# A chunked state-space layer and a gelu MLP on one core: how the first sequence's operands are loaded and turned, and where B by token comes from

## The chip, the cores and the metric

The kernel runs on one core of one Trainium2 chip. The metric is the time of one execution on the device in microseconds (us). The kernel before takes 120.17 us, the median of three runs (119.97 to 120.31).

## What is computed

Two layers follow each other. The first is a state-space scan over 4 sequences (b) of 768 tokens, with 8 heads (H) of width 32 (D) and a state of 16 (N) per head. It is computed in chunks:

```python
log_a = np.log(np.clip(a, 1e-06, 1.0))
for c in range(nc):
    cum = np.cumsum(la, axis=-1)
    L = np.exp(cum[:, :, :, None] - cum[:, :, None, :]) * causal
    M = np.einsum('bhin,bhjn->bhij', Cc, Bc) * L
    y_intra = np.einsum('bhij,bhjd->bhid', M, xc)
    y_inter = np.einsum('bhin,bhnd->bhid', Cc, state) * np.exp(cum)[..., None]
    y[:, :, sl] = y_intra + y_inter
    Bx = np.einsum('bhjn,bhjd->bhjnd', Bc, xc) * np.exp(cum[:, :, -1:] - cum)[..., None, None]
    state = np.exp(np.sum(la, axis=-1))[:, :, None, None] * state + np.sum(Bx, axis=2)
```

The second is an MLP over the 3072 tokens, with the 8 heads side by side as 256 features: `gelu_tanh(y @ w_in) @ w_out`, with w_in 256x2048 and w_out 2048x256. All inputs and the output are float32. The result does not depend on the chunk length; the kernel uses chunks of 128 tokens, 6 per sequence, 24 in all.

## The kernel before, in words

**Units.** The 24 chunks are taken as 13 units: chunk 0, chunk 1, and then pairs. Every function `f_...` issues the instructions of one step for one unit, and its steps are these.

- Decays. Products of `a` from a token to the end of its chunk are formed by a scan on VectorE (`f_R` for sequence 0 and the chunk ends of all, `f_scang` for sequences 1 to 3). B is multiplied by that product and C by its reciprocal (`f_mul0`, `f_mul`, `f_mulg`), so that no matrix of decays is needed.
- B and C are needed with (head, state) on the partitions: `bh` and `ch`. In sequence 0, PE transposes them (`f_T0` for chunk 0, L583; `f_T` for the rest, L604), and ACT copies them out of PSUM (`f_bh0`, `f_E`). In sequences 1 to 3 VectorE does it by its 32x32 block transpose (`f_Tg`, L543). `ce` is C twice, masked to even and odd heads (`f_ce0`, `f_F` L619, `f_Fg` L553).
- G (L659) is B times C, 128x128 for each head, in `gb`; M (L669) is its copy with the causal mask, bfloat16.
- B by token (`bn`) is needed with tokens on the partitions. In every sequence PE transposes `bh` back (`f_N`, L625) and ACT copies the result out (`f_bn`, L458).
- D (L680) is B by token times x, the chunk's addition to the state; S (L728, L730) carries the state on and SP (L737) spreads it out over a block mask `bmask`.
- Y (L702 from the carried state, L711 from M and x) is the layer's output; `f_yev` (L720) copies it to `xm`.
- s1 (L757) is the first stage of the MLP, `f_gelu` (L765) its gelu on ACT, s2 (L774) the second stage; `f_oev` copies the result out and `f_store` (L787) sends it. The last chunk's s2 is done in two halves (L792) in one tile `gb`.

x and the weights are cast to bfloat16 (`f_castx`, `f_wi`, `f_wo`, all through L458 to L462), mostly on GpSimd.

**Order.** The order of the work is not that of the code. Each step is a node with an engine, an estimated duration, the steps that it needs and a priority; `run_order` goes through them as if each engine ran in order, and issues them in the order found. PSUM is scarce: the two `hp` tiles are shared by s1, D and small products, `gb` by G, M and `f_N`, `yb` by Y and some s2. Where the plan has PE idle, before the first s2, `idle` puts products of a zero tile there (L1065).

**Loads.** All loads but two stand in one queue on SP, in this order: `a`; B and C of chunk 0 (64-byte rows); B and C of all of sequence 0 (384-byte rows); x of chunk 0; w_in, a quarter at a time, with x of chunk 1 and of chunks 2 and 3 between; w_out in four quarters; x of chunks 4 and 5; then for each of sequences 1 to 3 `a`, B, C (four loads each), and x. The stores are in the same queue.

```python
load_bc_n()
load_x_n(0)
load_w_n(0, 1)
load_x_n(1)
load_w_n(2, 3)
load_x_n(2)
load_w_n(0, 1, 2, 3, o=True)
load_x_n(3)
```

Of the kernel before, what the change touches and what calls it, by code (L numbers as in the profile page):

```python
# [31 lines left out]
def run_order(nodes, pools, hop=0.08, same=0.04, idle=None, wait=()):  # L32
# [64 lines left out]
    'f_clip(0, 256)': 308.538, 'f_R(0,)': -15.941, 'f_clip(256, 384)': -339.826, 'f_RT0()': 1159.49,  # L97
    'f_R(1,)': 367.141, 'f_recip0()': -323.896, 'f_mul0(1,)': -323.906, 'f_mul0(0,)': -35.176,
    'f_T0(1,)': 1123.21, 'f_T0(0,)': 1159.5, 'f_ce0()': -138.371, 'f_bh0()': 266.725, 'f_R(2,)': 330.337,
    'f_G(0,)': -91.981, 'f_pe()': -193.992, 'f_RT()': 1125.27, 'f_M(0, 0, 0, 2)': -285.936,  # L100
    'f_M(0, 0, 2, 4)': 367.131, 'f_pp()': 1125.26, 'f_recip()': 468.131, "f_castx(0, 'ACT')": 266.715,
    'f_mul(1,)': -194.002, 'f_pend()': 270.364, 'f_Y(0,)': 1119.78, 'f_yev(0,)': 209.42,
    'f_mul(0,)': -35.176, 'f_T(1,)': 1152.81, "f_wi(0, 0, 2, 'POOL')": 97.158,
    "f_E(0, 1, 'ACT', 21, 64)": 270.354, 'f_T(0,)': 55.447, "f_E(0, 1, 'ACT', 64, 128)": 272.36,
    'f_F(0, 128, 384)': 468.121, 'f_D(0,)': 1170.19, 'f_s1(0, 0)': 1244.43,
    "f_E(0, 0, 'ACT', 21, 64)": -152.035, 'f_F(0, 384, 768)': -343.397, "f_wi(1, 0, 2, 'POOL')": 106.043,
    "f_E(0, 0, 'ACT', 64, 128)": 102.425, 'f_S(0, 0)': -318.328, 'f_G(1,)': 1209.63, 'f_SP(0,)': -323.654,
    'f_gelu(0, 0)': 267.9, 'f_N(0,)': 1123.2, "f_castx(1, 'POOL')": 106.053, 'f_M(1, 0, 0, 4)': -287.074,
    'f_s1(0, 1)': 1244.44, "f_bn(0, 'ACT')": 270.405, 'f_D(1,)': 1119.09, 'f_gelu(0, 1)': 103.579,
    'f_G(2,)': 379.65, "f_wi(2, 0, 1, 'POOL')": -96.227, "f_wi(2, 1, 2, 'DVE')": 244.836,  # L110
    'f_S(1, 0)': 509.234, 'f_Y(1,)': 1167.76, 'f_SP(1,)': -318.348, 'f_s1(0, 2)': -68.513,
    'f_yev(1,)': -185.791, "f_wi(3, 0, 1, 'POOL')": 97.168, "f_wi(3, 1, 2, 'DVE')": -166.728,
    'f_gelu(0, 2)': 88.559, 'f_M(2, 0, 0, 4)': 468.111, 'f_s1(0, 3)': 256.892, 'f_s1(1, 0)': -5.424,
    'f_gelu(0, 3)': 841.948, 'f_M(2, 1, 0, 4)': 286.612, "f_castx(2, 'POOL')": 106.083,
    'f_gelu(1, 0)': 209.42, 'f_s1(1, 1)': 1244.44, 'f_D(2,)': -72.563, 'f_gelu(1, 1)': 310.499,
    'f_G(3,)': 1170.77, "f_wo(0, 'POOL')": -6.862, 'f_S(2, 0)': -86.636, 'f_s1(1, 2)': 1167.75,
    'f_SP(2,)': -328.534, 'f_S(2, 1)': -166.718, 'f_Y(2,)': 1125.08, 'f_gelu(1, 2)': -187.491,
    'f_SP(3,)': -95.439, "f_wo(1, 'POOL')": 106.093, 'f_s1(1, 3)': 39.343, 'f_M(3, 0, 0, 4)': 471.605,
    'f_yev(2,)': 310.489, "f_s2(0, 0, 0, 'o')": 1244.43, "f_s2(0, 0, 1, 'o')": 1149.98,
    'f_gelu(1, 3)': 43.879, "f_wo(2, 'POOL')": 71.86, 'f_s1(2, 0)': 262.608, 'f_M(3, 1, 0, 4)': -59.147,  # L120
    'f_s1(2, 1)': 1158.13, 'f_gelu(2, 0)': 316.947, "f_s2(0, 0, 2, 'o')": -169.949,
    "f_wo(3, 'POOL')": -209.595, 'f_gelu(2, 1)': 45.731, 'f_s1(2, 2)': 1170.19, 'f_s1(2, 3)': -203.565,
    'f_gelu(2, 2)': -95.091, "f_s2(0, 0, 3, 'o')": 1161.73, "f_castx(3, 'POOL')": 106.073,
    'f_gelu(2, 3)': -187.501, 'f_s1(2, 4)': -116.936, 'f_clipg(1,)': -328.524, 'f_scang(1,)': -182.29,
    "f_oev(0, 'ACT')": 316.957, 'f_s1(2, 5)': -331.499, 'f_gelu(2, 4)': 69.73, 'f_rT(1,)': 1150.59,
    "f_s2(1, 0, 0, 'o')": -206.245, 'f_qT(1,)': -105.019, "f_s2(1, 0, 1, 'o')": 281.291,
    'f_gelu(2, 5)': -281.439, 'f_D(3,)': -165.791, 'f_s1(2, 6)': 215.528, 'f_mulg(1, 0, 0, 3)': -276.921,
    "f_s2(1, 0, 2, 'o')": 348.67, 'f_S(3, 0)': -197.187, 'f_gelu(2, 6)': -234.888,
    "f_s2(1, 0, 3, 'o')": -86.131, 'f_SP(4,)': -161.739, 'f_s1(2, 7)': -124.52,
    'f_mulg(1, 0, 3, 6)': -104.486, "f_oev(1, 'ACT')": 253.329, 'f_Y(3,)': -102.426, 'f_store(0,)': 1122.82,  # L130
    'f_gelu(2, 7)': -70.863, 'f_Tg(1, 0, 0, 3)': -94.76, "f_s2(2, 0, 0, 'o')": -163.857,
    'f_Tg(1, 0, 3, 6)': -94.74, 'f_yev(3,)': -250.819, "f_s2(2, 0, 1, 'o')": -198.132,
    'f_mulg(1, 1, 0, 3)': -35.543, 'f_N(1,)': -102.426, "f_s2(2, 0, 2, 'o')": -88.02,
    'f_Tg(1, 1, 0, 3)': -42.833, "f_bn(1, 'ACT')": -84.712, 'f_s1(3, 0)': -86.121, 'f_Fg(1, 0, 3)': -153.974,
    'f_s1(3, 1)': -168.693, 'f_gelu(3, 0)': -281.449, 'f_mulg(1, 1, 3, 6)': -29.236,
    "f_s2(2, 0, 3, 'o')": 85.43, 'f_store(1,)': 1190.34, 'f_G(4,)': 280.653, 'f_gelu(3, 1)': 98.272,
    'f_Tg(1, 1, 3, 6)': -105.336, 'f_s1(3, 2)': 281.281, "f_oev(2, 'ACT')": 316.947,
# [115 lines left out]
def kernel(  # L253
# [68 lines left out]
    def load_bc(b, i):  # L322
        d = U[b]
        if "bc" not in d:
            d["bc"] = ld.tile([128, 2, H, R6 * N], FP32, name="bc_t")
# [777 lines left out]
```

## Time and profile before

| what | value |
|---|---|
| median of three runs | 120.17 us |
| profiled execution, its own time | 118.98 us |
| its span (first to last instruction) | 117.0 us |
| granted TensorE clock, mean | 0.995 of full speed |
| first s1 / first s2 on PE | 12.30 / 21.29 us |
| first G / G of chunk 1 / G of chunks 2 and 3 | 6.67 / 13.28 / 15.18 us |
| last product's end / last copy's end | 113.57 / 114.31 us |
| busy PE, DVE, ACT, POOL | 111.7, 71.2, 75.3, 18.1 us |

PE is TensorE, PEld its weight loads, DVE VectorE, ACT ScalarE, POOL GpSimd, SP the engine that issues most DMAs. A busy engine is one that runs any instruction, the zero products included. The profile page gives the busy share of each engine in 40 slices of 2.9 us, as digits in tenths. The chain of waits goes back from the last instruction to what released each one. In the timeline an instruction that waits for another engine inside its execution shows as a longer duration, not as idle time.

### The profile page before, as it was taken

The page shows a single profiled execution, that of the slowest core. Times are in us where ns is not written, and L with a number is a line of the kernel's source. Part 1 is how long each engine was busy: PE and PEld are TensorE (multiplying, and loading weights), DVE is VectorE, ACT ScalarE, POOL GpSimd, SP SyncE. Part 2 cuts the span into 40 slices and gives each one's busy share as a digit, 9 for nine tenths or more (in the row PEclk, how much of TensorE's full clock was granted, in tenths as well). Part 3 has the DMA queues.
Part 4 walks back from the last instruction along what each step waited for, and adds up shares of the span by engine and source line. Part 5 has one row for each costly group of instructions (what it writes and reads, how often), then busy time and mean ns, then how long its engine had stood idle before and what let it go on. Part 6 is the DMA issues. An engine that isn't in the chain of part 4 may idle for free.

```text
span 117.0 us, 3536 instructions
## 1 busy us (share of the span) xinstructions
PE 111.7 (96%) x1484; PEld 98.9 (85%) x1484; DVE 71.2 (61%) x161; ACT 75.3 (64%) x145; POOL 18.1 (16%) x38
## 2 busy tenths in 40 slices
PE   5899999999999999999999999999999999999980
PEld 5788778997987897998989899898989899999970
DVE  3787999939699996994999693291919000000100
ACT  4123756795765778687666859667777776676610
POOL 7303735640032003200510000000000000000000
PEclk9999999999999999999999999999999999999998
DMA  2998979968959497579611101101101101111111
GB/s 49 251 287 233 364 180 375 313 153 188 207 137 218 112 210 169 117 186 208 172 46 45 44 7 45 41 12 45 50 0 45 50 0 44 45 50 45 46 47 45
DMA packets 44251, 14.28 MB, mean 122 GB/s; under 512 B 39052, under 2 KB 42700, under 8 KB 44236
## 3 DMA queue, kind: packets, MB, share of 16 engines
q1 hardware_dynamic: 43148, 13.95, 48.4%
q10 hardware_dynamic: 1088, 0.11, 0.7%
q8 instruction: 11, 0.18, 0.6%
q14 instruction: 4, 0.03, 0.1%
HBM read 10.91 MB, written 3.15 MB: 120 GB/s over the span
## 4 chain that ended last, share of the span: by engine, by line
PE 87%; DVE 7%; POOL 2%; issue 1%; ACT 1%; POOLq 0%; DVEq 0%; ACTq 0%
PE hp L757 35%; PE o_ps L774 31%; PE gb L659 3%; PE yb L774 3%; DVE m L669 3%; PE yb L711 3%; PE yb L702 3%; PE o_ps L1065 2%; PE gb L792 2%; DVE ce L619 1%; PE hp L492 1%; PE gb L625 1%; DVE sp_new L737 1%; DVE w_in_sb L462 1%; PE hp L680 1%
## 5 line engine op out<-in xcount | busy, mean ns | idle before, releaser
L765 ACT ACTIVATE gT<-hp 128x512 bf16<-128x512 f32 x96 | 53.6, 596 | 20.0 <-PE hp L757 19.9
L757 PE MATMUL hp<-xm,w_in_sb 128*128 128x256 bf16 (+1 forms) x416 | 53.0, 267 | 0.0
L757 PEld LDWEIGHTS <-w_in_sb 128*128 128x128 bf16 x416 | 42.0, 115 | 3.3 <-issue 2.1
L774 PE MATMUL o_ps<-w_out_sb,gT 128*128 128x256 bf16 x336 | 44.4, 273 | 0.0
L774 PEld LDWEIGHTS <-gT 128*128 128x128 bf16 x368 | 35.8, 98 | 3.6
L669 DVE TENSOR_TENSOR m<-gb,tri 128x1024 bf16<-128x1024 f32 (+1 forms) x25 | 28.5, 1171 | 0.0
L783 DVE COPY o_sb<-o_ps 128x256 f32<-128x256 f32 x1 | 0.4, 425 | 18.5 <-ACT gT L765 18.5
L781 ACT ACTIVATE o_sb<-o_ps 128x256 f32<-128x256 f32 x20 | 7.7, 386 | 4.9 <-ACT gT L765 3.2
L737 DVE SCALAR_TENSOR_TENSOR sp_new<-s_new,pend,bmask 128x256 bf16<-128x256 f32 x20 | 10.3, 526 | 0.3
L1065 PE MATMUL o_ps<-wz 128*128 128x128 bf16 x75 | 8.9, 281 | 1.3 <-DVE warm L364 1.3
L460 POOL CAST x<-xs_t 128x512 bf16<-128x512 f32 x9 | 5.6, 654 | 27.6 <-DMA xs_t<-in_x_dram 18.1
L730 DVE SCALAR_TENSOR_TENSOR s_new<-s_new,pend,hp 128x64 f32<-128x64 f32 x16 | 4.5, 279 | 7.3 <-PE hp L680 4.4
L720 ACT ACTIVATE xm<-yb 128x512 bf16<-128x512 f32 (+1 forms) x13 | 7.3, 563 | 2.4 <-PE yb L711 2.2
L1065 PEld LDWEIGHTS <-wz 128*128 128x128 bf16 x75 | 6.9, 129 | 1.6 <-DVE warm L364 1.3
L711 PE MATMUL yb<-m,x 128*32 128x128 bf16 x192 | 6.3, 223 | 0.0
L702 PE MATMUL yb<-ce,sp_new 128*32 128x128 bf16 x160 | 5.3, 221 | 0.0
L659 PE MATMUL gb<-ce,bh 32*128 32x256 bf16 x96 | 5.2, 282 | 0.1
L533 DVE TENSOR_TENSOR bc<-bc_t,rr 128x192 bf16<-128x192 f32 x12 | 4.6, 435 | 1.0 <-DMA bc_t<-in_C_dram 0.9
L460 POOL CAST w_in_sb<-wf 128x512 bf16<-128x512 f32 x6 | 3.7, 636 | 8.4 <-DMA wf<-in_moe_w_in_dram 8.4
L460 POOL CAST w_out_sb<-wf 128x1024 bf16<-128x1024 f32 x4 | 4.2, 1040 | 2.4 <-DMA wf<-in_moe_w_out_dram 2.4
L711 PEld LDWEIGHTS <-x 128*32 128x32 bf16 x192 | 3.8, 97 | 0.8 <-issue 0.8
L702 PEld LDWEIGHTS <-sp_new 128*32 128x32 bf16 x160 | 2.9, 96 | 1.7 <-issue 1.6
(83 smaller groups left out, 67.3 us busy)
## 6 DMA issues: line engine op xcount, KB each, us to landing
out_dram<-o_sb SPq DMA_DIRECT2D x23, 128.0 KB, 1.8
xs_t<-in_x_dram SPq DMA_DIRECT2D x3, 768.0 KB, 6.6
wf<-in_moe_w_in_dram SPq DMA_DIRECT2D x4, 512.0 KB, 7.0
wf<-in_moe_w_out_dram SPq DMA_DIRECT2D x4, 512.0 KB, 6.4
bc_t<-in_B_dram SPq DMA_DIRECT2D x12, 96.0 KB, 2.8
bc_t<-in_C_dram SPq DMA_DIRECT2D x12, 96.0 KB, 2.3
x_t<-in_x_dram SPq DMA_DIRECT2D x6, 128.0 KB, 7.3
bc_t<-in_C_dram SPq DMA_DIRECT2D x1, 384.0 KB
```

Of the source, the lines that this page charges most:

```text
L460: nc.gpsimd.tensor_copy(out=o, in_=i)
L659: nc.tensor.matmul(out=gb[:, g, 256 * k:256 * k + 256], lhsT=bh_of(gc)[32 * g:32 * g + 32], rhs=ce_of(gc)[32 * g:32 * g + 32], start=True, ...
L669: nc.vector.tensor_tensor(out=MT[gc][:, g0:g1], in0=gb[:, g0:g1, 256 * k:256 * k + 256] .rearrange("p g (e t) -> p g e t", e=2), in1=tri_b ...
L702: nc.tensor.matmul(out=y4[32 * j:32 * j + 32, k, w], lhsT=sp[:, 32 * h:32 * h + 32], rhs=ce_of(gc)[:, h % 2], start=first(j), stop=False, ...
L711: nc.tensor.matmul(out=y4[32 * j:32 * j + 32, k, w], lhsT=X16[u][:, k, 32 * h:32 * h + 32], rhs=m[:, h // 2, h % 2, :], start=first(j), st ...
L720: nc.scalar.activation(xm[:, :, t0:t0 + n * Q].rearrange("p w (c t) -> p c w t", c=n), y4[:, 0:n], AF.Copy)
L737: nc.vector.scalar_tensor_tensor(out=sp_new.rearrange("p (g d) -> p g d", g=4), in0=state[("s", gc)].rearrange("p (o d) -> p o d", o=1).to ...
L757: nc.tensor.matmul(out=hp[:, j * nt:(j + 1) * nt], lhsT=w_in5[:, kc, fi // 4, fi % 4], rhs=xm[:, kc, t0:t0 + nt], start=(kc == 0), stop=(k ...
L765: nc.scalar.activation(gts[u][:, i * per:(i + 1) * per, 0:nt], hps.pop((u, i)).rearrange("p (j t) -> p j t", j=per), AF.Gelu_apprx_tanh)
L774: nc.tensor.matmul(out=ops[gc], lhsT=gts[u][:, fi, tt * Q:(tt + 1) * Q], rhs=w_out_sb[:, fi, :], start=(fi == 0), stop=(fi == NF - 1), ski ...
L781: nc.scalar.activation(o_sb, ops.pop(gc), AF.Copy)
L1065: nc.tensor.matmul(out=zb[:, 0:128], lhsT=wz[:, 0:128], rhs=wz[:, 0:128], start=True, stop=True)
```

## The change

It has four parts, and all steps are planned anew: new priorities, and a table `ENG` that lets copies, casts and products run on another engine than their first choice.

1. **Sequence 0 in two groups**, chunks 0 to 3 and chunks 4 and 5. For a group, `a` is loaded as 32 rows (8 heads of this sequence, then those that follow in memory) of 128 tokens per chunk. B and C are loaded with token 4p+r at partition p, so a row is 4 tokens of one head, 256 bytes. One scan, one 32x32 block transpose and one reciprocal on VectorE give the decays in that layout, and the products with B and C are split by heads over VectorE and GpSimd. PE transposes, and the copies out of PSUM put the tokens of C in order. For chunks 0 to 3, B's tokens stay in the order r, p, and the causal mask `triq` is made for that order.
2. **x of chunks 0 to 3** comes in two loads with rows of 512 bytes, in the layout of B, and is moved to the order r, p by PE with float32 products with a piece of the identity.
3. **B by token in sequences 1 to 3** is no longer transposed back on PE. GpSimd (in one case VectorE) multiplies B, as loaded, by its decays, and transfers from SBUF to SBUF put it on the partitions.
4. The rest: w_in quarters 2 and 3 in one load; the weights' casts in pieces of 512; the halves of the last product in two `hp` tiles; the state's decays of sequence 0 from a small product with `mq` and `selq`; the buffers of sequence 3 in the weights' staging tiles; `gT` in three wider tiles.

```diff
+    A0 = [(0, 4), (4, CPB)]
+    def load_bc0(k, i):
+        c0, c1 = A0[k]
+        src = (B, C)[i]
+        nc.sync.dma_start(out=bcq[0:32 * (c1 - c0), i],
+                          in_=bass.AP(tensor=src.tensor, offset=src.offset + c0 * Q * N,
+                                      ap=[[R * N, 32 * (c1 - c0)], [S * N, H], [1, R * N]]))
+    def load_xq(j):
+        nc.sync.dma_start(out=xq[64 * j:64 * j + 64].rearrange("p h r d -> p h (r d)"),
+                          in_=bass.AP(tensor=x.tensor, offset=x.offset + 2 * j * Q * D,
+                                      ap=[[R * D, 64], [S * D, H], [1, R * D]]))
...
-    idf = const.tile([64, 64], FP32, name="idf")
+    idf = const.tile([128, 128], FP32, name="idf")
...
+    triq = const.tile([128, Q], BF16, name="triq")
+    nc.gpsimd.memset(triq, 1.0)
+    for r in range(R):
+        t = triq[32 * r:32 * r + 32]
+        nc.gpsimd.affine_select(out=t, in_=t, pattern=[[1, Q]], compare_op=ALU.is_ge,
+                                fill=0.0, base=-r, channel_multiplier=-R)
+    mq = const.tile([128, 4], FP32, name="mq")
+    nc.gpsimd.memset(mq, 1.0)
...
+    def f_pe0(k):
+        p = slice(0, n0(k))
+        nc.vector.tensor_scalar(out=pe0[k][p], in0=mq[p], scalar1=a0c[k][p, 0:1],
+                                scalar2=r0[k][p, 0:1], op0=ALU.mult, op1=ALU.mult)
...
+    def f_mul0(k, i, h0, h1, eng):
+        p = slice(0, n0(k))
+        (nc.gpsimd if eng == "POOL" else nc.vector).tensor_tensor(
+            out=bq16(k)[:, i, :, h0:h1], in0=bcq[p, i, h0:h1].rearrange("p h (r n) -> p r h n", r=R),
+            in1=(r0T_of(k), q0T[k][p])[i][:, :, h0:h1].rearrange("p r (h o) -> p r h o", o=1)
+            .to_broadcast([n0(k), R, h1 - h0, N]), op=ALU.mult)
...
+    def f_xp(c):
+        T0[("x", c)] = t = (yb if c == 0 else next_hp())[:, 0:H * D]
+        rs = slice(32 * c, 32 * c + 32)
+        for r in range(R):
+            nc.tensor.matmul(out=t[32 * r:32 * r + 32].rearrange("p (h d) -> p h d", h=H), lhsT=idf[rs, rs],
+                             rhs=xq[rs, :, r], start=True, stop=True, tile_position=(32 * c, 32 * r),
+                             skip_group_check=True)
...
+    def f_bq(b, e, eng):
+        t = U[b]["bq"].rearrange("p r (c e) n -> p e r c n", e=2)[:, e]
...
+        (nc.gpsimd if eng == "POOL" else nc.vector).tensor_tensor(
+            out=t, in0=v, in1=w.to_broadcast([128, R, CPB, N]), op=ALU.mult)
+    def load_bn(b, g):
+        nc.sync.dma_start(out=d["bn"][:, 192 * g:192 * g + 192],
+                          in_=d["bq"][32 * g:32 * g + 32].rearrange("p r k n -> p r (k n)"))
...
     def f_s2h(h):
+        ops[("h", h)] = next_hp()[:, 0:128]
         for f in range(NF):
-            nc.tensor.matmul(out=gb[:, 2 * h, 0:128], lhsT=gts[NU - 1][:, f, Q:2 * Q],
+            nc.tensor.matmul(out=ops[("h", h)], lhsT=gts[len(BLOCKS) - 1][:, f, Q:2 * Q],
...
-        nn = add("PE", 0.34, f_N, b, deps=ts, prio=q + 15.6)
-        bb = add("ACT", 0.75, f_bn, b, "ACT", deps=[nn], prio=-45)
-        nn.takes("gram", bb)
...
+        bq = []
+        for e in range(2):
+            bq.append(any_of({"POOL": 0.95, "DVE": 0.55}, f_bq, b, e, deps=bl[(b, 0)] + [rt] + bq, prio=q - 0.5))
+        for n in bnl[b]:
+            n.deps += bq
```

The order in which the changed kernel issues its loads on SP is: `a` of chunks 0 to 3 (two of four on ACT's queue); C and B of chunks 0 to 3; `a` for the chunk ends; `a` of chunks 4 and 5 and x of chunks 0 to 3 in turn; w_in's first quarter, its second half, its second quarter; w_out's first two quarters; B and C, then x, of chunks 4 and 5; w_out's last two quarters; then sequence by sequence as before, each with its four transfers of B by token behind x and two stores.

On VectorE the order at the start is: setup, the clip, scan and block transpose of chunks 0 to 3, `f_pe0`, the reciprocal, half of the C product, half of the B product. On GpSimd the masks `tri`, `triq`, `mq` and `m8` come first, then the other halves of the two products, then the weights' casts.

## The prediction

> **What bounds the kernel now.** I read the page's busy shares and 40 slices first, then the chain of waits, then the timelines of the two ends, VectorE's and GpSimd's by themselves.
>
> ```profile
> PE 111.7 (96%) x1484; PEld 98.9 (85%) x1484; DVE 71.2 (61%) x161; ACT 75.3 (64%) x145; POOL 18.1 (16%) x38
> ...
> PE   5899999999999999999999999999999999999980
> ...
> DVE  3787999939699996994999693291919000000100
> ...
> DMA  2998979968959497579611101101101101111111
> ```
>
> Averages mislead here. PE counts as busy from 1.3 us on, but until the first second-stage product (21.29 us) it also runs 75 fill products on `wz` (L1065), which compute nothing. VectorE is the full engine in the first half of the slices, the DMA engines up to slice 20; after 40 us both have room and PE is alone. So there are two limits: a head up to about 21 us, set by loads and by VectorE's queue, and from there PE, by the sum of its work.
>
> ```profile
> 30.41 0.34 PE gb L625 x6
> ...
> 50.13 0.34 PE gb L625 x6
> ...
> 71.00 0.33 PE gb L625 x6
> ...
> 111.77 1.80 PE gb L792 x32
> 113.66 0.30 DVE o_sb L462
> 114.03 0.28 ACT o_sb L458
> ```
>
> This is the chain of waits, in order of time. From 21.45 us on it is PE without a hole, so what PE no longer does there is gained one for one. At the end both halves of the last product are followed by two copies in a row.
>
> **Part 1, N leaves PE.** In sequences 1 to 3 the change drops `f_N` (L625), six transposes each: 0.34 + 0.34 + 0.33 = 1.01 us off the chain, **-1.01**. Three evictions of 815 ns leave ACT, which is idle 19.9 us waiting for L757, so they give nothing. In their place come six products of 128x384 (five on GpSimd, one on VectorE) and twelve small SBUF transfers on SP's queue. The trace has no GpSimd product. Its casts bound it: 422 ns for 256 elements per partition, 609 for 512, so about 0.52 for 384 from below; one that reads two operands at the cost of two casts, 1.04, from above. I take 0.9, nearer the upper end, since it reads two tensors. The first pair is needed by D of chunks 6 and 7 (at 35.95 before); B of that sequence lands by 27.4, so the pair is done by 30. Behind it on SP stand four transfers, then the loads of sequence 2, which SP issued from 33.10 on anyway. A transfer out of SBUF lands 1.8 us after issue (the stores), one of a like size behind a big load 3.4 (C of sequence 1: last issue 27.2, landed 30.75). So B by token is there between 32 and 34: **0**, and up to +1 if it comes later, since D stands in PE's queue and all stage products wait behind it. GpSimd is 16% busy, so its own 5 us are hidden.
>
> **Part 2, the tail.** The last product's halves go to two `hp` tiles instead of one `gb`. Today the first half is computed at 112.67 (half of 1.80), but its copy waits to 113.66, the second to 114.03, and the second store is issued at 113.98 + 0.41 = 114.39. With separate tiles the first copy and store lie beside the second half; the second copy runs 113.66 to 113.94 and its store goes out at 114.01: **-0.38**.
>
> **Part 3, the head.** Sequence 0's chunks 0 to 3 now come as tokens 4p+r from one chain, instead of chunk 0 alone and the rest later.
>
> Gone: R's transposes by 24 small float32 products (1.46 us, 7.07 to 8.53), two products of 0.95 on VectorE, 12 transposes, and C's masks (L619: 1.65 us from 11.69 to 13.34, stretched). These hold G of chunk 1 until 13.28.
>
> Added before the first G: the setup on GpSimd grows by `triq` (a fill of 0.20 and four selects of 0.29, the row of `tri`) and `mq` (0.70, the row of `m8`, 3.49 to 4.19). With `tri` ready at 3.54, and about 0.1 more for the larger `idf`, `mq` is ready at about 3.65 + 0.20 + 1.16 + 0.70 = 5.7. VectorE's next instruction behind the transposed decay is the product with `mq` (`f_pe0`), and the reciprocal that the C product needs stands behind it: 5.7 + 0.15 + 0.33 (between 0.21 for 8 and 0.45 for 48 columns) = 6.2. Then each of C and B is multiplied half on VectorE (0.44 for 256 elements, carried on from 0.28 for 128 and 0.37 for 192), half on GpSimd. Do the halves overlap? The timelines of the two engines:
>
> ```profile
> 15.05 0.42 DVE L462 CAST w_in_sb<-wf 128x512 bf16<-128x512 f32 x1
> 15.69 0.48 DVE L737 SCALAR_TENSOR_TENSOR sp_new<-s_new,pend,bmask 128x256 bf16<-128x256 f32 x1
> 16.09 0.83 DVE L462 CAST w_in_sb<-wf 128x512 bf16<-128x512 f32 x1
> ...
> 20.31 1.12 DVE L737 SCALAR_TENSOR_TENSOR sp_new<-s_new,pend,bmask 128x256 bf16<-128x256 f32 x1
> ```
> ```profile
> 15.99 0.65 POOL L460 CAST w_in_sb<-wf 128x512 bf16<-128x512 f32 x1 [1.50 <-DMA wf<-in_moe_w_in_dram]
> ...
> 20.11 1.04 POOL L460 CAST w_out_sb<-wf 128x1024 bf16<-128x1024 f32 x1 [0.30 <-DMA wf<-in_moe_w_out_dram]
> ```
>
> The same VectorE cast takes 0.42 alone and 0.83 beside a GpSimd cast; the same two-tensor operation 0.48 and 1.12. Both end 0.28 after the GpSimd cast ends (16.64, 21.15): the one stood still for the other. So I count the halves one after the other: 4 products, two of 0.44 and two of 0.7 (between 0.42, one cast, and 0.84, two), 2.3 us, of which restarts save a little: C and B are done at about 8.3. Four transposes 0.43 (6 take 0.65), copy to `bh` 0.28 and hops: G of chunk 0 at about 9.3, against 6.67 now. That is 2.6 late; overlapped halves would make it 1.5 late.
>
> From there it gains: chunks 1 to 3 need no further loads or transposes, x is there, and G of chunk 1 follows Y of chunk 0 (about 11.5 against 13.28). VectorE sets the pace. Its queue from the first clip to the end of chunk 3's M holds, by rows, M 2 x 0.65 and 3 x 1.17, four S 1.0, four SP 1.8, decays and reciprocals of two groups 2.4, products 0.9, PSUM copies 1.2, R and clip 1.1, a weight cast 0.42: about 13.6 us; from 4.2, with 0.5 for the wait on `mq`, 1 for GpSimd and 1 for hops it ends near 20, now 19.19. Meanwhile the first w_out cast can run 1 to 3 us earlier than 18.76, because the two x loads ahead of it (x of chunks 1 to 3, 128-byte rows; GB/s fall to 175 in 14 to 16) are gone, so PE has three or four second-stage groups (0.44 each, 1.3 to 1.75) to do in its gaps. Against this stand after 20 us the transposes, N and copies of chunks 4 and 5, about 1.3 on PE, which before were behind it, and fewer groups of the first stage.
>
> New on PE: x of four chunks is turned by 16 float32 products of 32x256, four per chunk in four column groups. No row has this. Lower bound: a bfloat16 product of 256 columns adds 0.109, and four column groups run beside each other (8 of Y in 0.11), with two records per float32 product (as in L483): 0.22; float32 records are at least 61 ns each (24 in 1.46), 8 make 0.49. Upper: not overlapped and at half pace per record 1.75 a chunk. I take 0.6, nearest the 61 ns row, and 2.4 us in all fit between 8 and 14 us, where PE runs fill now.
>
> Sum of the head: later by 2.6 at G, by about 1 at Y of chunk 0, ahead at chunk 1, level with PE's work by 21: between **-1.0** (weights and second stage early, halves overlap) and **+2.5** (VectorE's queue late all the way). I take **+0.8**, near VectorE's count (20.0 against 19.19).
>
> **Sum.** -1.01 - 0.38 + 0.8 = **-0.6 us**. The profiled execution has a span of 117.0 and a time of 118.98; so 116.4 and 118.4. The median of the runs shown is 120.17, 1.2 above that execution; carried over: **119.6 us**.
>
> **The Trainium skill.** "SBUF — State Buffer", section "SBUF: two separate sides", says that VectorE and GpSimd share one pair of ports under an exclusive lock, also against VectorE operations with two SBUF inputs, and that the loser waits for the whole instruction. It speaks against this change; the two pairs of rows above agree (0.83 for 0.42, 1.12 for 0.48). By the rule every GpSimd product of B by token also stops VectorE, which is the rival "lock" below. "GPSIMD Engine Reference", section 3, gives 4497 ns for a two-tensor add of 2048 float32; an estimate from that page is 0.84 us for 384 elements and 0.56 for 256; with it the sum would be some 0.2 lower. No run here shows it yet.
>
> **Rivals.**
> *Lock.* Ten GpSimd products (about 4.5 + 3.5 us) stop VectorE in the head and while sequence 1 is prepared (26 to 33 us), where it is already 9 tenths busy. For: the rows above; 0.6 lost at 20.31 alone. Against: from 21 us PE has stages of units 1 and 2 to fill in, and M of unit 4 came at 33.27 for a Y at 38. Price +0.5 to +0.9 over the forecast: 120.2. Chance 0.2, no change.
> *x by float32 does not overlap* (ends slower). The four column groups share their rows and run in turn: at 1.2 to 1.75 a chunk 2.4 to 4.6 us more PE time between 8 and 14 us, just ahead of the first D and Y; fills there leave some 1.5. Price +1.5 to +3, 121 to 122.5, from about 0.9 us a chunk on. For: no row shows float32 at this width. Against: Y's 14 ns a product. Chance 0.15.
> *Late head or B by token late for D of chunk 6*, +1.2 to +2: 120.8 to 121.5. Chance 0.13.
> *The head gains too*, -1.0 instead of +0.8: 118.0 to 118.6. For: w_out early. Chance 0.14.
> Forecast (119.6, itself 119.1 to 120.0): 0.38.
>
> So faster by over 0.3% (0.36 us, about what a measurement of this kernel tells from no change; below 119.8): 0.14 and most of the forecast, 0.36, together **0.50**; within it **0.21** (lock and the forecast's edge); slower **0.29**. Range **118.4 to 121.4**.
>
> **What would show it.** L625 gone for sequences 1 to 3 and nothing of PE in its place; the second copy of the last product within 0.1 of PE's end; G of chunk 0 at 9 to 9.5 with VectorE's wait on GpSimd before `f_pe0`; the GpSimd halves not beside VectorE's; PE without fill or hole from about 21 us. I am wrong if G comes by 8, if the four products of one chunk of x take over 1 us, or if PE waits for a `bn` transfer.

## The result and the profile after

The changed kernel takes 127.0 us (median of 4 runs, 126.43 to 127.41), the kernel before 120.07 beside it: ratio 1.058, interval 1.052 to 1.064, slower by 6.9 us where 0.6 us less was forecast. The profiled executions lie further apart than the medians (spans of 125.6 and 117.0 us), since that of before was one of its quickest and that of the changed kernel the slowest of its four. The traces are compared on the spans, the experiments by their ratios to the kernel before on the same chip.

The page of the changed kernel, the rows that answer to those of before, with the clock's row:

```profile
PE 114.3 (91%) x1462; PEld 96.3 (77%) x1462; DVE 80.6 (64%) x180; ACT 74.4 (59%) x143; POOL 26.5 (21%) x54
...
PE   5576999987999899859989999999999999999990
...
DVE  3698487939999699729689989969384642001000
...
PEclk9985555999999999999999999999999999999998
DMA  1989995999962999366971022110111011110111
```

TensorE (PE) now has slices that are not full up to the twenty-first (66 us), and the clock's row falls to a half from 9 to 22 us. To see what that costs, cut the execution at 24 us, behind the head. Busy time of each engine in three stretches (start:end, length, then PE, PEld, DVE, ACT, POOL, clock, DMA share, GB/s), first before, then after:

```profile
24.00:64.00 40.00, 40.00 (x544) 35.01 (x543) 34.09 (x79) 28.93 (x55) 6.41 (x11) 1.00 0.76 158
64.00:108.00 44.00, 44.00 (x572) 39.82 (x571) 16.63 (x32) 32.04 (x62) 0.00 (x0) 1.00 0.11 35
108.00:126.00 18.00, 5.56 (x67) 5.11 (x65) 0.72 (x2) 2.71 (x6) 0.00 (x0) 0.91 0.07 23
```
```profile
24.00:64.00 40.00, 36.31 (x511) 30.51 (x510) 31.68 (x71) 26.14 (x51) 9.60 (x14) 1.00 0.86 175
64.00:108.00 44.00, 43.71 (x596) 39.08 (x596) 31.36 (x60) 28.04 (x53) 3.16 (x4) 1.00 0.14 43
108.00:126.00 18.00, 14.63 (x150) 13.72 (x148) 0.42 (x1) 9.48 (x20) 0.00 (x0) 0.97 0.14 45
```

Before, PE has 89.56 us of work left at 24 us and no hole. After, it has 94.65 us left, though the transposes N are gone, and 3.69 + 0.29 = 4.0 us of holes. So the head is late by 5.1 us, 4.0 us are lost in holes, and behind the last product the changed kernel needs 125.6 - 122.65 = 2.95 us instead of 3.43: 5.1 + 4.0 - 0.5 = 8.6 us, the difference of the spans.

**The head.** The same eight products of 128 columns show the clock better than its row, which stands at full speed before 9 us too. PE's timeline of before, of after, and of two experiments below (e3, e2):

```profile
12.30 1.04 PE L757 MATMUL hp<-xm,w_in_sb 128*128 128x128 bf16 x8
...
14.03 0.61 PE L757 MATMUL hp<-xm,w_in_sb 128*128 128x128 bf16 x8
```
```profile
11.67 1.08 PE L714 MATMUL hp<-xq,idf 32*32 32x256 f32 x8
...
21.38 1.06 PE L866 MATMUL hp<-xm,w_in_sb 128*128 128x128 bf16 x8
...
22.34 0.64 PE L866 MATMUL hp<-xm,w_in_sb 128*128 128x128 bf16 x8
```
```profile
16.36 0.61 PE L864 MATMUL hp<-xm,w_in_sb 128*128 128x128 bf16 x8
```
```profile
8.76 0.63 PE L714 MATMUL yb<-xq,idf 32*32 32x256 f32 x8
...
11.58 0.63 PE L714 MATMUL hp<-xq,idf 32*32 32x256 f32 x8
...
12.31 0.96 PE L714 MATMUL hp<-xq,idf 32*32 32x256 f32 x8
...
14.80 1.08 PE L714 MATMUL hp<-xq,idf 32*32 32x256 f32 x8
...
21.64 1.06 PE L866 MATMUL hp<-xm,w_in_sb 128*128 128x128 bf16 x8
```

Eight take 1.04 us at half speed and 0.61 at full speed. Before, PE reaches full speed between 12.3 and 14 us; after, at 22.3 us, with PE busy without a gap from 12 us on.

**The holes.** PE's timeline of after, the lines behind 24 us with 0.4 us or more of idle time ahead of them (in brackets, with what ended it); then SyncE's queue (start, and how long the issues and the waits between them took):

```profile
29.09 0.60 PE L866 MATMUL hp<-xm,w_in_sb 128*128 128x256 bf16 x4 [1.10 <-DVE ce L695]
...
43.05 1.03 PE L866 MATMUL hp<-xm,w_in_sb 128*128 128x256 bf16 x8 [0.44 <-DVE s_new L839]
...
52.16 0.60 PE L866 MATMUL hp<-xm,w_in_sb 128*128 128x256 bf16 x4 [0.54 <-ACT gT L874]
...
56.49 0.63 PE L866 MATMUL hp<-xm,w_in_sb 128*128 128x256 bf16 x4 [1.40 <-DVE s_new L839]
...
64.29 1.03 PE L886 MATMUL o_ps<-w_out_sb,gT 128*128 128x256 bf16 x8 [0.43 <-DVE o_sb L526]
```
```profile
11.18 10.12 SPq L381 DMA_DIRECT2D xe<-in_x_dram  x2
21.47 1.10 SPq L518 DMA_DIRECT2D wf<-in_moe_w_out_dram  x2
...
32.14 3.15 SPq L896 DMA_DIRECT2D out_dram<-o_sb  x2
35.39 3.24 SPq L739 DMA_DIRECT2D bn<-bq  x4
38.67 0.59 SPq L395 DMA_DIRECT2D at<-in_a_dram  x1
```

SyncE stands 10 us in the two short-row loads of x of chunks 4 and 5, then waits for two stores, then issues the four moves of B by token (`bn`), and only then `a` of sequence 2, at 38.67 instead of 33.10. VectorE has its clip of `a` ahead of the state update (`s_new`), and PE waits for that (the holes of 0.44 and 1.40).

### The profile page after: what moved, and what is told of

Same layout as the page of the kernel before. It is cut to its first block, busy times and chain, and to the rows that moved or that the text cites. A ratio compares the mean times of both kernels' runs of the same rounds, so it can differ in the third digit from the quotient of the medians.

```text
span 125.6 us, 3557 instructions
## 1 busy us (share of the span) xinstructions
PE 114.3 (91%) x1462; PEld 96.3 (77%) x1462; DVE 80.6 (64%) x180; ACT 74.4 (59%) x143; POOL 26.5 (21%) x54
## 4 chain that ended last, share of the span: by engine, by line
PE 72%; ACT 6%; DMA 6%; SPq 5%; POOL 4%; DVE 3%; issue 2%; POOLq 0%; ACTq 0%
PE hp L866 30%; PE o_ps L886 24%; DMA at<-in_a_dram 6%; SPq L739 4%; PE gb L769 3%; PE yb L886 3%; ACT ce L693 3%; PE hp L714 2%; PE yb L821 2%; ACT gT L874 2%; PE yb L812 2%; PE o_ps L1213 2%; PE hp L902 1%; DVE ce L695 1%; POOL triq L452 1%
## 5 line engine op out<-in xcount | busy, mean ns | idle before, releaser
L886 PE MATMUL o_ps<-w_out_sb,gT 128*128 128x256 bf16 x336 | 45.7, 273 | 0.4 <-DVE o_sb L526 0.4
L779 DVE TENSOR_TENSOR m<-gb,tri 128x1024 bf16<-128x1024 f32 x20 | 23.7, 1215 | 0.1
L1213 PE MATMUL o_ps<-wz 128*128 128x128 bf16 x58 | 7.6, 294 | 1.3 <-DVE warm L420 1.3
L522 ACT ACTIVATE o_sb<-o_ps 128x256 f32<-128x256 f32 x15 | 5.8, 385 | 3.1 <-PE o_ps L886 2.0
L522 ACT ACTIVATE xm<-yb 128x512 bf16<-128x512 f32 (+1 forms) x9 | 4.9, 549 | 3.2 <-PE hp L790 1.8
L731 POOL TENSOR_TENSOR bq<-bc,at 128x384 bf16<-128x384 f32 x4 | 3.7, 948 | 11.0 <-DMA bc<-in_C_dram 7.3
L524 POOL CAST w_out_sb<-wf 128x512 bf16<-128x512 f32 x7 | 4.4, 654 | 4.9 <-DMA wf<-in_moe_w_out_dram 4.9
L526 DVE CAST xm<-yb 128x512 bf16<-128x512 f32 x4 | 2.8, 688 | 3.7 <-PE yb L821 2.6
L779 DVE TENSOR_TENSOR m<-gb,triq 128x1024 bf16<-128x1024 f32 (+1 forms) x5 | 4.9, 1002 | 0.2 <-PE gb L769 0.2
L524 POOL CAST x<-wf 128x512 bf16<-128x512 f32 x3 | 2.1, 741 | 12.4 <-DMA wf<-in_x_dram 12.4
```

Source lines behind the costliest of these rows:

```text
L522: nc.scalar.activation(o, i, AF.Copy)
L524: nc.gpsimd.tensor_copy(out=o, in_=i)
L779: nc.vector.tensor_tensor(out=MT[gc][:, g0:g1], in0=gb[:, g0:g1, 256 * k:256 * k + 256] .rearrange("p g (e t) -> p g e t", e=2), in1=(triq ...
L886: nc.tensor.matmul(out=ops[gc], lhsT=gts[v][:, fi, tt * Q:(tt + 1) * Q], rhs=w_out_sb[:, fi, :], start=(fi == 0 and gc != 1), stop=(fi == ...
L1213: nc.tensor.matmul(out=zb[:, 0:128], lhsT=wz[:, 0:128], rhs=wz[:, 0:128], start=True, stop=True)
```

## The experiments

Gains within the changed kernel are given against it as (its ratio - 1.058) x 120.3 us; the intervals are about 0.5 to 0.8 us to either side. Kernels timed apart that differ in one placement (e7, e17) came out 1.1 us apart, so nothing finer is concluded. In the diffs, `move(k, m)` puts step k of the written order directly ahead of step m, `extra(n, m)` puts n products of zeros there.

**Four parts of the changed kernel, one at a time** (e1 to e4).

```
e1  + move("load_a(2,)", "load_bcg(1, 0, 0)"); move("load_a(3,)", "load_bcg(1, 0, 0)")
e2  + for n, k in ((14, "f_pp0(0,)"), (3, "f_T0(0, 1)"), (2, "f_T0(0, 0)"), (5, "f_G(0,)"), (3, "f_N0(0, 1)")):
    +     extra(n, k)
e3  f_xp: - for r in range(R): nc.tensor.matmul(out=t[32*r:32*r+32] ..., lhsT=idf[rs, rs], rhs=xq[rs, :, r], ...)
          + for r in range(5): nc.tensor.matmul(out=t, lhsT=wz[:, 0:128], rhs=wz[:, 0:256], ...)
e4  load_xe: - in_=x[0, :, c*Q:(c+1)*Q, :].rearrange("h p d -> p h d")
             + in_=bass.AP(..., offset=x.offset + (c-4)*Q*H*D, ap=[[H*D, Q], [D, H], [1, D]])
```

> The changed kernel with the loads of the decays (a) of sequences 2 and 3 issued directly behind that of sequence 1, ahead of the moves of B by token; nothing else differs. Theory Q (SyncE's queue: the load of a stands behind four moves that wait for GpSimd and two stores, VectorE waits for a with the state update queued behind it): both waits of VectorE for a, at 42 and at 56 us, go, and with them the TensorE holes of 0.6, 0.7 and 1.4 us before 64 us: 127.0 becomes 124.3 to 125.2 us. Rival R (B and C of the next sequence stand behind the same moves and are as late as a): the waits move to them and the time stays above 126.4 us.

Measured 125.24 us, ratio 1.039 (1.035 to 1.043): 2.2 us less. The holes at 43 and 56 us are gone. Theory Q holds. The next wait of this kind, on the chain of waits of this kernel, is x of sequence 2, at the end of the same queue, issued at 43.89 and landed 6.75 us later.

> The changed kernel with 27 more products of zeros on TensorE in the gaps of the first 11.5 us (14 ahead of the chunk-end product, 3 and 2 ahead of the two transposes, 5 ahead of G of chunk 0, 3 ahead of the first B by token): TensorE is then as little idle there as in the kernel before. Theory C (the gaps of 3.1 us between 5 and 11.5 us hold TensorE's clock down): eight 128-wide products of the first matrix take 0.6 us from about 14 us instead of from 22.3 us, the work between 14 and 22 us takes half its time, and the end comes 2 to 4.5 us earlier, 122.5 to 125 us. Rival X (it is the small products of the stage, not the gaps): the clock comes up at the same 22 us and the time stays within 0.6 us of 127.0.

125.92 us, ratio 1.045 (1.041 to 1.049): 1.5 us less, more than the rival and less than theory C allowed, and not as theory C has it. The lines of e2 above show it: the clock is up at 8.8 and 11.6 us (four products of x in 0.63), falls while the next are done, and stays low until 22.5 us. The gaps had kept it low until 11 us; what keeps it low from then on is something else. So the 1.5 us do not come from the clock behind 13 us: PE's holes behind 24 us are 2.7 us instead of 4.0, and why is not shown.

> The changed kernel with the float32 products that bring x of chunks 0 to 3 into order (32 rows by 32 columns of the array at a time) replaced by five products of zeros on the whole array into the same tile, of about the same time (1.07 us at the low clock); x of these chunks is then taken as zero, which this kernel leaves out. Theory X (products on a sixteenth of the array do not raise TensorE's clock): the clock comes up by 14 to 17 us instead of 22.3, and the time falls by 2 to 4.5 us. Theory C (gaps) and theory L (the clock is not what bounds this stage, the loads and copies are): within 0.6 us of 127.0.

125.64 us, ratio 1.044 (1.040 to 1.047): 1.7 us less, and PE at full speed from its first product of the stage, at 16.36 us. Products of zeros on the whole array, of the same time at half speed, do not lower the clock; the float32 ones on 32 rows by 32 columns do. Theory X holds for the clock; for the time it had 2 us or more. PE's work left at 24 us falls by 1.9 us only, because other things are then late: PE waits 0.56, 0.73 and 0.32 us between 17 and 21 us for copies, the gelu and the second matrix.

> The changed kernel with x of chunks 4 and 5 of sequence 0 loaded as 1 KB rows from another place (as many bytes, an eighth of the packets; the values are those of other tokens, which this kernel leaves wrong). Theory L (SyncE stands 10.1 us in the two issues of these short-row loads, and the last two quarters of the second weight matrix, a, B, C and x of sequence 1 are late for it): these loads are issued by 2.4 us earlier, the transfers of sequence 1 land as much earlier, and the end comes 0.8 to 2.5 us earlier. Rival C (TensorE at half clock bounds everything up to 26 us, so earlier loads wait): within 0.5 us of 127.0.

126.39 us, ratio 1.050 (1.046 to 1.054): 1.0 us less, its interval overlapping that of the changed kernel. SyncE stood 5.3 us in these loads instead of 10.1.

**The products of x alone, on the kernel before** (e18).

```
e18  + def xtra(): for r in range(R): nc.tensor.matmul(out=zb[32*r:32*r+32, 0:256] ..., lhsT=idf[0:32, 0:32],
     +                 rhs=XF[0][0:32, 0], start=True, stop=True, tile_position=(0, 32*r), ...)
     + ahead of f_Y(0) (in place of the fill there), f_D(0), f_G(1), f_D(1): xtra
```

> The kernel before, computing all of the reference, with the change's float32 products of x added and their results not used: four times four products of 32 rows by 32 columns of the array by 256, ahead of Y of chunk 0 (in place of 8 products of zeros), of D of chunk 0, of G of chunk 1 and of D of chunk 1. The prediction's step (2.4 us that fit where TensorE runs fill): 0 to 0.8 us above the kernel before. Theory X (they hold TensorE's clock down behind them, which the head of the kernel before feels too): the first matrix's products of 128 columns take 1.04 us per eight until 18 us or later instead of until 13 us, and the time is 1.5 to 3.5 us above, 121.7 to 123.7 us. Rival: their own time lies on the path but the clock is up by 15 us all the same: 0.8 to 1.5 us above.

124.51 us, ratio 1.040 (1.033 to 1.046): **4.8 us slower than the kernel before**, more than theory X had. PE's timeline of this kernel, then its busy time behind 24 us:

```profile
20.72 1.49 PE L1065 MATMUL o_ps<-wz 128*128 128x128 bf16 x12
22.00 1.72 PE L757 MATMUL hp<-xm,w_in_sb 128*128 128x128 bf16 x16
...
23.95 0.61 PE L757 MATMUL hp<-xm,w_in_sb 128*128 128x128 bf16 x8
```
```profile
sum 102.00, PE 94.92 PEld 84.75 DVE 54.57 ACT 67.52 POOL 7.34; mean PE 31.64 PEld 28.25 DVE 18.19 ACT 22.51 POOL 2.45
```

The clock comes up at 23 us instead of 14, and PE has 94.92 us left at 24 us, near the changed kernel's 94.65. The twelve fill products that took 0.83 us before take 1.49. So with the head of before, its G at 6.7 us and its loads, these sixteen products alone make about as much lateness as the changed head has.

The lateness has two parts. The products of the first matrix that started at 17.00 before start at 22.00 here, and PE is busy without a hole from 9 to 24 us. Of these 5.0 us the products of x themselves take 4.0, less 1.0 for the eight products of zeros whose place they take; the other 2.0 are work that ran at full speed before and now runs at half. At full speed the products of x would take some 2.3 us (an estimate, 0.57 each four in e2). And e18 keeps the order of before, with 26 more products of zeros, 2.6 us, in the same stretch, which a new plan could leave out. So 4.8 us is rather an upper price: in the changed kernel, e3 gets 1.7 back.

**The head of the changed kernel mended** (e9 to e11, e15).

```
e9   triq and tri built in f_tri(), emitted ahead of f_T0(0, 1), behind the POOL products
     + move("f_F0(0, 1, 1, 4)", "f_F0(0, 0, 1, 4)"); move("f_xp(0,)", "f_xpe(0,)")
e10  + xq16 = bfloat16 copy of xq by nc.gpsimd.tensor_copy, 64 partitions at a time
     f_xp: - lhsT=idf[rs, rs], rhs=xq[rs, :, r]   + lhsT=ident[rs, rs], rhs=xq16[rs, :, r]
e11  e1 + e9 + e10
e15  e11; + load_bc0(1, 0), load_bc0(1, 1) ahead of load_wi(2); f_mul0(1, ...) ahead of f_wo(0, 0);
     + f_T0(1, .), f_E0(1, 4, 6), f_F0(1, ., 4, 6) ahead of f_s1(0, 1); stores of chunks 0, 1, 3 behind load_bn
```

> The changed kernel with the head reordered and nothing else: the two triangular masks are built by GpSimd behind its products for chunks 0 to 3 and not ahead of them (1.9 us), of the three copies of C that ScalarE and VectorE make one after the other for chunks 0 to 3 the long one stands behind those of chunk 0, and G of chunk 0 stands ahead of the first move of x. Theory H (G of chunk 0 at 10.5 us instead of 6.7 us sets how late everything behind it is): G of chunk 0 at 8.7 to 9.3 us and the end 1.0 to 1.8 us earlier. Rival (from 12 us on TensorE is busy at the low clock or the weights are late, so that an earlier G waits there): G as early, the end by less than 0.4 us.

125.74 us, ratio 1.044 (1.036 to 1.052): 1.7 us less; G of chunk 0 at 9.15 us.

> The changed kernel with x of chunks 0 to 3 cast to bfloat16 by GpSimd first (two more instructions of about 1 us) and moved by bfloat16 products of 32 rows by 32 columns instead of float32 ones. Theory X (the 4.3 us of float32 products on a sixteenth of the array keep the clock low until 22.4 us): the products of a chunk of x take 0.3 us, the clock is up by 13 to 18 us and the end is 1.0 to 2.0 us earlier, as with products on the whole array. Rival (products on a part of the array keep it low whatever they take; or the casts delay the weights' casts on GpSimd): clock up after 20 us, less than 0.6 us.

125.93 us, ratio 1.045 (1.038 to 1.052): 1.6 us less. A chunk's products take 0.40 us and full speed comes at 19.7 us: less time on small products, a clock that is up earlier, though not as early as expected. Whether it is the float32 format, the small part of the array or both that holds the clock, no run separates: float32 products on the whole array were not tried.

> The changed kernel with three edits at once, computing all of the reference: a of sequences 2 and 3 issued early, the head reordered, x cast to bfloat16 before it is moved. If the three losses add (1.9 to 2.2, 1.0 to 1.8 and 1.0 to 2.0 us): 121.5 to 123.5 us where the kernel before takes 120.5. If what is saved ahead is lost at SyncE's queue (two stores and four moves that wait for one another from 32 us on, and the short-row loads of 10 us ahead of them): 124 to 126 us.

125.23 us, ratio 1.035 (1.027 to 1.044): 2.7 us less, where the three parts alone gave 2.2, 1.7 and 1.6. The chain of waits of this kernel names what comes in their place:

```profile
11.22 10.34 DMA bcq<-in_C_dram
...
21.82 2.36 POOL b L669 x3
24.23 0.30 PE hp L678 x4
24.55 0.75 ACT bh L526
25.30 0.58 ACT ce L697
25.91 0.80 DVE ce L699
26.75 0.60 PE hp L870 x4
```

C of chunks 4 and 5 lands 10.3 us after its issue, three GpSimd products and three copies follow one another, and PE has a hole of 1.1 us. VectorE's copy of C waits for ScalarE's, so here two engines do not make these copies faster than one.

> The changed kernel with the three edits of the earlier run (a early, head reordered, x cast to bfloat16) and three more, computing all of the reference: B and C of chunks 4 and 5 loaded ahead of the second half of the first weight matrix and worked on ahead of the casts of the second matrix (they had landed at 21.6 us, 10.3 us after their issue, and TensorE waited for the copies made from them at 26 us), and the stores of chunks 0, 1 and 3 behind the moves of B by token. If these are what is left: no hole at 26 us, 121.0 to 123.5 us where the kernel before takes 120.5. If the weights, later by what now stands ahead of them, set the pace: 124 to 126 us, as without the three.

125.44 us, ratio 1.041 (1.034 to 1.049): no better than e11. The hole at 26 us shrinks to 0.4 us, with one of 0.5 for the copy of B ahead of it, and PE waits 1.2 us at 21.95 for the second matrix, whose loads are now behind. The rival holds.

**Edits together** (e5, e6). e5 is e1 + e3, e6 is e1 + e2 + e3 + e4.

> The changed kernel with both edits at once: the loads of a of sequences 2 and 3 issued early, and the float32 products of x of chunks 0 to 3 replaced by products of zeros on the whole array (x of these chunks taken as zero, left out). Alone they gave 1.9 and 1.7 us. If the two losses are independent (low clock in the head, queue of SyncE later on): 3.3 to 3.9 us below the changed kernel, 123.3 to 124.0 us where the kernel before takes 120.5. Rival (the transfers of sequences 1 and 2 set the pace of 30 to 56 us anyhow, whatever the head does): no more than 2.4 us below, 125.0 us or more.

126.19 us, ratio 1.045 (1.040 to 1.050): 1.6 us less, no more than either alone. In this run SyncE waited for the stores until 37.5 us, the moves of B by token were issued from 37.6, and PE waited 0.5 and 0.4 us for them directly. The rival holds.

> The changed kernel with all four edits at once: a issued early, products of zeros in place of those of x of chunks 0 to 3 (left out), 1 KB rows in place of 128 B rows for x of chunks 4 and 5 (values wrong), and 27 products of zeros in the gaps of the head. If what was found so far (queue, clock, short rows) explains the loss: 120.8 to 122.3 us where the kernel before takes 120.5. If something else of the size of 2 us or more is left (the copies of C into token order with their TensorE hole at 27.5 us, the late G of chunk 0): 122.5 to 124 us.

124.64 us, ratio 1.036 (1.030 to 1.041): 2.7 us less, outside of both ranges. Behind 24 us a hole of 1.1 us, the copies of C (28.7 us), and one of 0.4 (61.3 us) are left. Ahead of it PE waits 2.1 us at 19.6 us for ScalarE's gelu, which stands behind a cast of the first matrix whose load came late.

**B by token** (e7 and e17 undo it in the changed kernel, e12 in e11; e13, e14, e16 put it alone into the kernel before).

```
e7, e17, e12  - f_bq(b, e), load_bn(b, g)    + six transposes of bh into one hp tile, one ScalarE copy to bn
e13  kernel before: - f_N(b), f_bn(b), b > 0  + f_bq(b, 0), f_bq(b, 1) on GpSimd; load_bn(b, 0..3) ahead of load_a(b + 1)
e14  e13 and e8; load_bn ahead of the stores of chunks 0 and 3    e16  e13, e8 and e1
```

> The changed kernel with B by token of sequences 1 to 3 made by six TensorE transposes and a ScalarE copy each, as in the kernel before, instead of GpSimd products and moves between parts of SBUF; the rest of the order is kept. The prediction's term (the transposes cost TensorE 1.0 us, the moves nothing): 127.7 to 128.3 us. Theory Q (the moves hold SyncE's queue and what stands behind them; 2 to 3 us of TensorE holes hang on it): 1.0 to 2.0 us below the changed kernel, 125.3 to 126.5 us.

126.89 us, ratio 1.051 (1.047 to 1.055): 0.8 us less, between the two expectations. In this kernel the transposes of sequence 1 overwrite a tile of the first matrix before its gelu has read it, so some values of chunks 4 and 5 are wrong.

> The changed kernel with B by token of sequences 1 to 3 by TensorE transposes and ScalarE copies, once more, with the transposes of sequence 1 placed so that no tile of the first matrix is written before it has been read; all of the reference is computed. It leaves the new head and tail alone against the kernel before. If the head is nearly all of the loss, as the earlier run of this gave: ratio to the kernel before 1.046 to 1.056. If the misplaced transposes had shortened or lengthened that run: outside of it.

127.22 us, ratio 1.060 (1.056 to 1.064), outside of what was expected: no gain. So with the new head it makes no difference that can be told how B by token is made; the new head, with the tail, is by itself as slow as the whole change.

> The kernel of the run before this one, and in addition B by token of sequences 1 to 3 by TensorE transposes and ScalarE copies as in the kernel before (the GpSimd products and the moves between parts of SBUF are gone), computing all of the reference. It tells what the moves cost once the head is mended. Theory Q (SyncE's queue and the moves set 32 to 56 us): 0.5 to 2 us below the run before. Rival (they cost nothing once a is early): 0.7 to 1.2 us above it, for the transposes on TensorE.

125.26 us, ratio 1.039 (1.032 to 1.046), beside 1.035 for e11: the same within the intervals. Neither side shown.

> The kernel before with one part of the change alone: B by token of sequences 1 to 3 by GpSimd products and moves between parts of SBUF, the moves of sequence 1 and 2 ahead of the load of a of the next sequence, as the change has them, those of sequence 3 ahead of the store of chunk 9; the transposes on TensorE and the ScalarE copies are gone. The prediction's term: 1.0 us below the kernel before, 119.5 us. Theory Q: the moves are issued from 33.1 us, behind two stores that SyncE waits for until then, the state update of chunks 6 and 7 at 36 us and the load of a of sequence 2 wait for them: 0 to 1.5 us above it, 120.5 to 122 us.

122.12 us, ratio 1.015 (1.009 to 1.020): 1.8 us slower than the kernel before. Two costs of the change stand in its timelines. GpSimd's products of B run just when VectorE makes its own:

```profile
27.78 1.82 POOL L656 TENSOR_TENSOR x_t<-bc_t,at 128x384 bf16<-128x384 f32 x2 [1.56 <-DMA bc_t<-in_B_dram]
27.87 1.95 DVE L534 TENSOR_TENSOR bc<-bc_t,at 128x192 bf16<-128x192 f32 x2
29.74 0.27 DVE L750 SCALAR_TENSOR_TENSOR s_new<-s_new,pend,hp 128x64 f32<-128x64 f32 x1
```

The same two VectorE products took 0.64 us before (27.40). The Trainium skill, "SBUF — State Buffer", section "SBUF: two separate sides", has the one engine wait for a whole instruction of the other; these lines agree. The state update behind them starts 1.8 us later than before, and PE has a hole of 0.43 us at 30.06. The second cost is the queue, on the chain of waits (pieces called issue, of 0.05 us and less, left out):

```profile
33.58 0.65 SPq L662
34.29 0.59 SPq L662
34.93 0.60 SPq L662
35.57 0.60 SPq L662
36.21 3.35 DMA at<-in_a_dram
39.58 0.03 DVE at L504
39.73 0.23 DVE s_new L748
39.98 0.29 DVE s_new L750
40.31 0.60 PE hp L777 x4
```

`a` is issued 2.6 us later behind the four moves, and PE's hole is 1.04 us. Together these two holes are 1.5 us, against 1.0 us of transposes that PE saves: 0.5 of the 1.8 us. The trace has two more holes, ahead of the first product of the change (27.78):

```profile
17.44 1.09 PE L777 MATMUL hp<-xm,w_in_sb 128*128 128x128 bf16 x16 [0.42 <-POOL w_in_sb L461]
...
25.71 0.60 PE L794 MATMUL o_ps<-w_out_sb,gT 128*128 128x256 bf16 x4 [0.73 <-POOL w_out_sb L461]
```

There PE waits for weights that land later than in the trace of before, with the same loads in the same order. Nothing that the change does had run by then, so the rest of the 1.8 us is not explained.

> The kernel before with two parts of the change: the two halves of the last chunk's product in the rotating tiles, and B by token of sequences 1 to 3 by GpSimd and moves, but the moves stand ahead of the stores for which SyncE waits anyhow (of chunks 0 and 1, and of chunk 3), and not behind them. If the place in SyncE's queue is what the moves cost: the 1.0 us of the transposes and the 0.5 us of the tail are both gained, 118.8 to 119.4 us, ratio 0.987 to 0.992. Rival (the moves or GpSimd beside VectorE cost as much as the transposes wherever they stand): 119.7 to 120.3 us, as with the tail alone (0.995).

121.57 us, ratio 1.011 (1.007 to 1.014): still slower than the kernel before. SyncE now waits for the GpSimd products instead of the stores, the moves take it until 35.9, the stores follow, and `a` is issued at 37.05. Both sides of the expectation fell: the moves cost in either place.

> The kernel before with the tail in the rotating tiles, B by token of sequences 1 to 3 by GpSimd products and moves behind the stores as the change has them, and the loads of a of sequences 2 and 3 directly behind that of sequence 1, so that no load of a waits for the moves. Theory Q in its narrower form (what the moves cost is the late a: a hole of 1.0 us before 40 us with this part alone): the hole goes, and what is left against the kernel before is the transposes (1.0 us) and the tail (0.5 us) gained and 0.4 to 1.0 us lost to GpSimd beside VectorE: 118.9 to 119.8 us where the kernel before takes 120.2. Rival (whatever stands behind the moves, a or B and C, is late): 120.3 to 121.6 us.

122.16 us, ratio 1.014 (1.010 to 1.019). Behind 32 us PE has no hole, as it should be if the late `a` made the one before 40 us; but PE is later by then and could hide such a hole. The three loads of `a` hold SyncE 4.8 us at 20 us, where the one load of before held it 3.7. B of sequence 1 is issued 1.8 us later, VectorE's products of it meet GpSimd's (1.69 us for two), and one hole of 2.8 us ends at 31.8. The result lies on the rival's side, beyond its range.

**The tail alone** (e8): on the kernel before, `f_s2h` and `f_oevh` use `next_hp()` tiles in place of `gb[:, 2 * h]`.

> The kernel before with one part of the change alone: the two halves of the last chunk's product go into the two rotating tiles of the first matrix instead of two quarters of the G tile. By the change's traces the time behind the last product falls by 0.38 to 0.48 us: 0.3 to 0.5 us below the kernel before, ratio 0.996 to 0.9975. Rival (the copy or the store, not the tile, sets the end): within 0.1 us of it.

120.03 us beside 120.53, ratio 0.995 (0.991 to 0.998): 0.5 to 0.6 us less, about what was expected. It is the one version here that beats both kernels.

## Why the prediction was wrong

The parts, each put alone into the kernel before: the products of x +4.8 us, B by token +1.8, the tail -0.6, together 6.0 of 6.9 us. That the sum comes near is no proof, since the parts do not add here: with B by token undone the changed kernel is as slow (e17), and without the products of x it gains 1.7 (e3), not 4.8.

- **The step that failed is "New on PE: x of four chunks ... 2.4 us in all fit between 8 and 14 us, where PE runs fill now", and with it the head's +0.8.** The size of one chunk's products was near (0.63 us at full speed, 0.6 taken). That is in part luck: of the rows it was read from, the 61 ns were taken at half speed (eight products beside them take 1.04 at 9.01) and the 0.109 at full. What had no term is the clock. At half speed a chunk takes 1.08 us, and what follows runs at half speed for some 9 us longer: together 4.8 us in e18, 1.7 back in e3. Nor was there room for 2.4 us: between 8 and 14 us the kernel before runs twelve products of zeros, 1.4 us, and the prediction's own rival has "some 1.5". Its own "wrong if" was met: 1.08 us for a chunk. The rival "x by float32 does not overlap" had the right place, from 0.9 us a chunk on, and ended on the right side; its mechanism (products in turn) was not it, and its price (1.5 to 3) was too low.
- "B by token **0**" and the -1.01 for N: alone it is +1.8 instead of -1.0, of which the waits named in e13's trace explain +0.5. B's GpSimd product was sized well (0.93 us on average, 0.9 taken), and the moves land 2.0 us after issue (1.8 to 3.4 taken). Missed were the order on SyncE (the moves are issued at 35.4 to 38.6 in the changed kernel, since stores stand ahead of them, and `a` stands behind) and the lock at the moment when VectorE multiplies B of the same sequence. The rival "lock" had this mechanism, at 0.5 to 0.9.
- G of chunk 0: 9.3 foreseen, 10.49 measured. `mq` was 0.4 us later (6.10), and the copies of C into token order came out in turn and long: 1.12, 0.50 and 0.54 us before G. That the halves of the products lie one after the other was right: 0.43 us alone, 0.84 beside GpSimd. It is worth up to 1.7 us (e9). VectorE, by whose count the head was to end near 20, ends chunk 3's M at 22.9.
- "PE without fill or hole from about 21 us" was a sign of being right, and 4.0 us of holes came. For the copies of C of chunks 4 and 5 the prediction has 1.3 us of PE's work and no wait; they make a hole of 1.1 us (29.09). The late `a` makes 1.8 more, and e1 without them is 2.2 us quicker.
- "The first w_out cast can run 1 to 3 us earlier than 18.76": it ran at 20.2. Its load was issued at 8.2 instead of 12.1 and landed 12 us later; what held it is not shown. The short-row loads did not vanish, they became two that stand behind it and hold SyncE for 10 us; with 1 KB rows in their place it ran at 19.6 (e4), with the short rows kept at 19.7 (e1).
- The tail, -0.38: 2.95 us instead of 3.43 behind the last product, -0.48, and -0.6 by e8. Right.

Taking out one of these parts of the changed kernel gives 1.0 to 2.2 us (B by token nothing, e17), taking out several no more than 2.7 (e6, e11). In the traces another wait then stands in the place of the one that is gone: G at 10.5 us, C of chunks 4 and 5 at 21.6, the second matrix, SyncE's queue. They are named by the traces of e5, e11 and e15; that each hides the next is argued from them. Not settled is which of them would have to go together to give the whole 6.9 us back.

## What to carry to other kernels

Cut the execution behind the head and compare TensorE's work left and its holes: two numbers say how much of a loss is lateness and how much is waiting, before any cause is named. Idle-looking room on TensorE that is filled with zeros may be what raises its clock (27 more zeros brought it up at 8.8 us in e2); put small products there only after measuring a product of the main stage behind them. A DMA that is added to an in-order queue is priced by what stands behind it, and a move in the queue has to be measured: other loads moved past it gained 2.2 us in one kernel (e1), nothing that can be told in another (e16).

## What the runs showed of the hardware

- Sixteen float32 products of 32x256 on 32 by 32 parts of the array, 4.3 us, held TensorE at half speed for some 9 us longer (e18: full at 23 instead of 14 us), with the array busy without a gap; five products of zeros on the whole array in the place of each four did not (e3), and with bfloat16 products (1.6 us in all) full speed came at 19.7 us (e10). The Trainium skill, "TensorE: Matmul & The Clock Gate", section "Part 1: The HAM clock gate (the "warmup" mystery)", has full speed after about 3.4 us of sustained activity; here 10 us of gapless work, small products among it, did not bring it (after, 12 to 22 us), so the measurement decides. That activity is weighed by how much of the array works is argued from e3 and e18, not shown; the float32 format is a rival that no run excludes.
- The clock's row is no proof: in e18 it stands at full speed throughout, while eight products take 1.05 us at 19.9 and 0.61 us at 23.95.
- A move between parts of SBUF held SyncE's queue 0.55 to 0.6 us each, and four delayed the next load by 2.6 us.
- ScalarE copies out of PSUM that scatter 128 columns in strides took 0.54 us, 384 columns 1.09 and 1.12 us (ce, L693).
